# Memory attention and a gated MLP on one core: the attention transposes of pairs 1 to 3 done on VectorE from 32x32 blocks

## The chip, the cores and the metric

One NeuronCore of a Trainium2 chip. The metric is device time in microseconds (us) of one execution: TensorE (PE in the profile, with its weight loads as PEld), VectorE (DVE), ScalarE (ACT), GpSimd (POOL) and SyncE (SP, which issues the DMAs here) run side by side and wait for each other by semaphores.

## The reference, cut to what matters

```python
# q, k, v: [8, 8, 576, 64]   phi: [8, 8, 576, 32]   (batch, head, sequence, .)
a = exp(phi - max(phi, axis=2));  a = a / (sum(a, axis=2) + 1e-9)
k_m = einsum('bhsm,bhsd->bhmd', a, k)            # 32 memory slots per head
v_m = einsum('bhsm,bhsd->bhmd', a, v)
scores = q @ k_m.T / 8
attn = exp(scores - max);  attn = attn / (sum + 1e-9)        # [.., 576, 32]
x = (attn @ v_m)  as [4608, 512]                  # heads side by side
xn = x / sqrt(mean(x*x) + 1e-6) * rms_g
out = (silu(xn @ w_gate) * (xn @ w_val)) @ w_out  # 512 -> 1536 -> 512
```

## The kernel before, in words

The 8 batches are 4 pairs (`pr` 0 to 3). `x` is never formed: the weights are first multiplied by `v_m` (`vw_steps`, tile vp), and the result is multiplied by the normalised attention weights themselves (`gv_steps`, tiles pg and pv, three products of high and low halves for precision); silu and product follow, and `out_steps` multiplies by w_out into po and adds into the output tile acc. The MLP runs as 24 units of (pair, sixth of the 1536 columns), each in two slices: pair 0's first four sixths, then pairs 0 and 1 mixed, then pairs 2 and 3. These matmuls are the main stream on TensorE, from some 80 us on.

For each later pair (1 to 3) the attention has to be made ready beside that stream, in two stages:

- `attend_steps(pr, s)`, four per pair (`s`: two heads of both batches). `fetch` (L660) loads q with four DMAs, 64 partitions each, rows of 64 floats, a token on a partition. `turn` transposes 9 blocks of 128x128 on TensorE against the identity (L671, tile qtp, in runs of 4, 4 and 1), and ScalarE copies each run from PSUM to qT (L677). `score` multiplies by `k_m` (L689, tile S); max, subtraction, exponential, sum and division follow on VectorE, ScalarE and GpSimd; `put` (L730) writes the 128x576 weights to a scratch tensor in HBM with one DMA.
- `x_steps(pr)`. `fetch` (L935) loads the scratch back in three pieces of 4, 4 and 1 tiles of 64 tokens (tile ain). `turn` transposes two 128x128 blocks of each tile on TensorE (L763, tile tp, 18 per pair), `copy` brings them to the tile at, on ScalarE or VectorE by a bit list `ON_SCALAR` (L773). Then per tile `mm` (L855, xp) and `square` (L867), which reads both xp and the rows ain, give the mean of squares; `fin` makes the reciprocal root on VectorE, `spread` brings it across (L783, rp) and scales at (L791), and ScalarE and GpSimd split at into ath and atl, which `gv_steps` reads.

Pair 0 takes another way (`q_steps`, `score_steps`, L585, and L763 with the tile first) that needs no scratch. The PSUM tag "o" (two banks) holds qtp, S, tp, xp, rp and also po of the main stream. The SBUF tags qr, qT, ex of the pool `sl` have one buffer each; `x_steps` uses the same three for its pieces.

Everything is cut into some 2940 small steps (`parts`), and the list `ISSUE` at the top of the file, made by a planner, says in which order they are issued. Each engine and SP's queue work in that order, so a step's place in the list is its place in the queue of its engine; there is no other priority. SP waits at a DMA until its buffer is free, and all that is listed behind it waits with it.

Of the kernel before, what the change touches and what calls it, by code (L numbers as in the profile page):

```python
# [28 lines left out]
ON_SCALAR = (21, 28, 14, 13)  # L29

ISSUE = [
    34, 36, 27, 35, 28, 33, 10, 0, 11, 229, 12, 1, 13, 2, 14, 3, 15, 4, 30, 5, 17, 29, 16, 18, 6, 898, 7, 41,
    19, 8, 20, 31, 9, 21, 22, 42, 32, 23, 43, 905, 24, 25, 44, 48, 37, 58, 26, 45, 59, 46, 49, 230, 39, 38,
    243, 75, 899, 115, 900, 40, 76, 47, 50, 51, 240, 902, 77, 60, 903, 53, 231, 52, 61, 232, 908, 85, 242, 54,
    62, 906, 86, 55, 923, 95, 65, 63, 87, 241, 66, 64, 68, 907, 67, 96, 909, 70, 56, 127, 910, 930, 78, 88,
    901, 948, 79, 116, 97, 80, 904, 913, 89, 69, 57, 81, 98, 90, 105, 82, 118, 91, 83, 233, 71, 119, 84, 99,
    117, 234, 106, 92, 151, 100, 120, 93, 101, 235, 94, 107, 152, 139, 72, 108, 102, 924, 128, 109, 153, 110,
    129, 103, 130, 121, 73, 111, 104, 140, 131, 112, 236, 154, 925, 132, 113, 122, 155, 114, 265, 133, 123,
    156, 279, 237, 141, 134, 142, 124, 165, 143, 157, 135, 144, 933, 125, 136, 126, 74, 171, 145, 164, 244,
    163, 137, 158, 138, 166, 172, 245, 911, 146, 266, 147, 173, 159, 169, 238, 912, 246, 239, 1270, 174, 277,  # L40
    148, 247, 170, 175, 276, 1271, 149, 167, 931, 150, 278, 926, 927, 248, 1273, 176, 168, 160, 177, 928, 196,
    202, 195, 197, 249, 932, 161, 162, 198, 250, 934, 200, 252, 929, 251, 203, 1272, 267, 178, 199, 268, 253,
    201, 179, 254, 269, 184, 255, 935, 916, 270, 914, 936, 180, 185, 204, 256, 181, 188, 937, 207, 1274, 205,
    182, 949, 915, 1295, 257, 917, 183, 206, 190, 258, 918, 191, 259, 189, 192, 955, 919, 261, 271, 260, 186,
    263, 1276, 262, 264, 208, 272, 187, 193, 1279, 951, 273, 280, 950, 194, 1275, 1281, 281, 1277, 1280, 1278,
    274, 209, 920, 275, 210, 1296, 211, 216, 952, 217, 282, 1282, 212, 214, 953, 1298, 218, 223, 213, 973,
    954, 283, 215, 219, 445, 221, 1297, 224, 220, 222, 921, 225, 226, 227, 228, 956, 1286, 284, 285, 958,
    1299, 957, 286, 959, 1285, 974, 287, 960, 1290, 1287, 980, 961, 976, 1310, 1283, 975, 1289, 289, 1288,
    290, 288, 1301, 977, 1291, 978, 1312, 446, 291, 1300, 938, 979, 293, 447, 292, 1292, 448, 1302, 1304, 449,
    294, 981, 450, 1314, 464, 451, 982, 1293, 295, 984, 296, 1338, 985, 983, 939, 1284, 452, 963, 297, 1339,  # L50
    1315, 1294, 986, 1303, 453, 1306, 1305, 1340, 941, 299, 1341, 454, 987, 1307, 300, 455, 940, 1308, 1342,
    298, 1311, 942, 465, 943, 1343, 466, 1313, 998, 944, 1316, 456, 1363, 966, 1317, 457, 1345, 1309, 467,
    945, 1344, 469, 1348, 946, 483, 458, 1357, 470, 459, 1318, 1347, 999, 460, 947, 1320, 461, 468, 462, 964,
    1322, 965, 1321, 463, 1346, 967, 968, 1326, 1000, 1359, 1005, 1323, 1002, 1001, 1353, 1003, 1364, 1023,
    1004, 1324, 1349, 962, 1366, 922, 1327, 969, 1354, 471, 1319, 1365, 1350, 1367, 1355, 1325, 1356, 1006,
    472, 474, 1008, 1007, 1358, 522, 1009, 1026, 1010, 1368, 1351, 473, 1030, 1011, 1360, 1378, 1370, 475,
    1024, 476, 484, 1012, 1025, 1372, 485, 1027, 486, 1361, 1028, 488, 1406, 487, 988, 1029, 489, 502, 1330,
    1352, 477, 1328, 1331, 1362, 1031, 478, 1407, 1334, 1329, 479, 480, 1409, 481, 989, 1332, 1335, 1032, 482,
    1033, 1408, 1336, 991, 990, 1333, 992, 993, 1369, 1337, 1034, 1048, 1373, 1035, 493, 994, 1371, 1013,
    1410, 490, 1374, 301, 1375, 1383, 491, 1036, 995, 492, 1380, 1411, 1376, 494, 996, 1037, 970, 1379, 1049,  # L60
    503, 1381, 1413, 971, 1382, 1051, 495, 507, 1431, 1050, 972, 1016, 1377, 1384, 1415, 997, 1014, 1385, 508,
    1015, 504, 505, 1052, 1386, 1412, 1017, 1053, 1388, 1055, 1054, 496, 1416, 506, 1018, 1432, 1390, 1073,
    1019, 1421, 1387, 1417, 1056, 1414, 497, 1426, 1434, 1058, 498, 1389, 499, 1418, 500, 1433, 1419, 1422,
    1423, 1074, 1057, 1425, 501, 1059, 1392, 1060, 1427, 1076, 1391, 1080, 1061, 1435, 1098, 1424, 1420, 1474,
    1428, 1393, 512, 1075, 1475, 509, 513, 1077, 1446, 514, 1081, 1078, 1396, 1083, 1038, 1079, 1436, 1082,
    510, 511, 1397, 1398, 1084, 1085, 515, 1394, 1063, 1086, 1477, 516, 1062, 1399, 1437, 517, 518, 1402,
    1448, 1395, 519, 1039, 1476, 1438, 1400, 1439, 520, 1478, 1087, 1064, 1403, 1066, 1441, 1040, 1429, 1065,
    1483, 1042, 521, 1043, 1440, 1041, 1067, 1404, 1401, 1442, 1443, 523, 1068, 1102, 548, 1044, 1447, 1088,
    1479, 561, 1430, 1045, 1451, 1444, 1449, 1481, 1445, 302, 1450, 524, 1046, 1452, 1480, 1020, 525, 1489,
    1103, 1021, 1047, 1405, 528, 1482, 526, 1453, 1022, 529, 1499, 1454, 527, 1104, 1105, 1484, 1106, 1485,  # L70
    1500, 1107, 1458, 1069, 1486, 1109, 530, 1459, 1108, 1091, 1490, 1501, 1089, 1456, 1491, 1502, 1487, 1503,
    1494, 1488, 531, 1112, 1457, 532, 1090, 534, 1092, 1493, 533, 535, 1093, 549, 1495, 555, 1455, 550, 1127,
    1504, 556, 312, 1094, 1492, 553, 1496, 551, 1100, 1497, 536, 1542, 554, 537, 1110, 538, 552, 539, 1460,
    540, 541, 1543, 542, 1111, 1506, 543, 544, 1545, 545, 1508, 546, 1461, 1128, 557, 1498, 1510, 559, 1113,
    1509, 558, 1129, 562, 1114, 1505, 563, 1134, 1115, 564, 547, 560, 1116, 1544, 1462, 1507, 565, 566, 314,
    567, 578, 1511, 1463, 1514, 1512, 579, 1513, 1464, 1546, 580, 1472, 582, 581, 1137, 1130, 568, 1131, 1135,
    1465, 1516, 1473, 1468, 569, 1132, 570, 1117, 1133, 1466, 313, 1136, 571, 1469, 572, 1470, 573, 574, 575,
    1138, 1518, 1070, 1515, 1071, 1520, 1095, 1519, 576, 577, 1139, 1467, 1096, 1142, 1471, 584, 1517, 303,
    1567, 1521, 304, 1522, 585, 1524, 1568, 1152, 305, 583, 1569, 1570, 1526, 1120, 1525, 1571, 1140, 588,
    1528, 586, 1527, 589, 1141, 590, 1529, 1610, 587, 591, 306, 1530, 307, 592, 594, 593, 1118, 1557, 1143,  # L80
    1531, 1144, 1558, 595, 1523, 1547, 1534, 308, 1562, 315, 309, 1532, 1146, 1549, 1147, 1145, 1119, 1559,
    1551, 1156, 1121, 337, 1122, 1560, 1181, 1123, 1535, 1553, 1548, 1561, 1550, 1533, 1552, 1563, 1576, 1554,
    1555, 316, 1611, 1556, 1572, 1157, 1612, 1613, 1573, 310, 1574, 1614, 317, 311, 1564, 1635, 338, 1578,
    1565, 318, 1577, 1566, 319, 1582, 351, 1148, 320, 321, 1586, 348, 322, 324, 325, 323, 350, 1575, 1588,
    1579, 1587, 326, 1580, 1097, 327, 329, 1615, 328, 1584, 1581, 349, 330, 1583, 332, 331, 1072, 1585, 1619,
    333, 1589, 1636, 339, 1616, 340, 1638, 341, 1637, 334, 335, 1184, 342, 1630, 336, 343, 1617, 1159, 1540,
    1639, 1536, 1541, 344, 1618, 1158, 1538, 1160, 345, 346, 1625, 1590, 1539, 1101, 347, 1537, 1620, 1099,
    1161, 352, 373, 1678, 1627, 1621, 1163, 1182, 1622, 353, 1210, 1623, 1640, 1624, 1644, 354, 1183, 1646,
    1185, 1626, 1591, 1186, 1629, 1628, 1171, 1187, 355, 1642, 1154, 1679, 356, 357, 1654, 596, 358, 360,
    1166, 361, 359, 1641, 362, 1681, 363, 365, 1592, 364, 1680, 1682, 1606, 1643, 1593, 1631, 1632, 1598,  # L90
    1607, 1645, 1599, 1600, 1647, 1594, 1601, 1633, 366, 1634, 1595, 1650, 1596, 1652, 368, 1164, 367, 1597,
    1703, 369, 1648, 370, 371, 1604, 1649, 1165, 1651, 1605, 372, 597, 1653, 1655, 1167, 598, 1162, 599, 1683,
    600, 1168, 1602, 1656, 672, 1169, 1704, 1685, 1705, 1693, 1603, 1657, 1174, 601, 1608, 615, 602, 1706,
    1707, 1687, 1684, 1188, 1689, 1609, 1170, 1746, 1686, 1149, 1658, 1150, 603, 1172, 606, 604, 1695, 1688,
    1124, 1151, 605, 607, 1698, 1125, 608, 1690, 616, 1697, 1659, 609, 1708, 617, 610, 618, 1694, 619, 611,
# [1160 lines left out]
```

## Time and profile before

| what | value |
|---|---|
| median of 3 runs (lowest, highest) | 824.86 us (822.37, 826.59) |
| the profiled execution | 823.65 us, span of its instructions 821.9 us |
| busy share of the span | PE 96%, PEld 82%, DVE 57%, ACT 45%, POOL 29% |
| DMA packets, bytes | 98622, 119.99 MB |

The page gives busy times by engine, the chain of work that ended last (followed back from the end through what each piece waited for), groups of instructions by line, and DMA issues. The trace answers by window, by line, by tile, and in order of time. "x4" is a count; "idle" is the time an engine stood still before an instruction.

### The profile page before, as it was taken

What the parts mean: (1) busy time and instruction counts of PE and PEld (TensorE: products, weight loads), DVE (VectorE), ACT (ScalarE), POOL (GpSimd) and SP (SyncE); (2) the same over time, 40 slices, a digit from 0 to 9 for tenths busy, and PEclk for the clock granted to TensorE, in tenths of its full rate; (3) what the DMA queues carried; (4) which work ended last, traced back from release to release, by engine and by line L of the source; (5) the groups of instructions that cost most, each with busy time, mean ns of one, the idle gap of its engine ahead of it and who ended that gap; (6) DMA issues with size and microseconds to landing.
All of it is one profiled execution on the core that took longest, in us unless ns stands there. A gap on an engine that the chain in (4) does not pass through costs nothing.

```text
span 821.9 us, 19112 instructions
## 1 busy us (share of the span) xinstructions
PE 787.4 (96%) x7930; PEld 670.8 (82%) x7930; DVE 466.9 (57%) x1048; ACT 366.2 (45%) x704; POOL 238.3 (29%) x203
## 2 busy tenths in 40 slices
PE   3769999999999999999999999999999999999998
PEld 2657878887888888888888888888888888888886
DVE  5688677988763565566546353456544431443443
ACT  1657788654556654332435346532332333332221
POOL 0143545435432333222422212130422122221211
PEclk9789999999999999999999999999999999999999
DMA  9953797756383743554146461741231242131114
GB/s 323 372 179 106 186 256 234 246 189 211 124 295 73 200 143 88 152 173 137 53 136 211 141 159 44 182 141 52 78 110 57 92 155 98 45 116 52 53 28 152
DMA packets 98622, 119.99 MB, mean 146 GB/s; under 512 B 47204, under 2 KB 63976, under 8 KB 98536
## 3 DMA queue, kind: packets, MB, share of 16 engines
q1 hardware_dynamic: 98536, 118.78, 46.6%
q8 instruction: 62, 1.02, 0.5%
q14 instruction: 24, 0.20, 0.1%
HBM read 93.19 MB, written 25.56 MB: 144 GB/s over the span
## 4 chain that ended last, share of the span: by engine, by line
PE 84%; DMA 6%; ACT 3%; DVE 3%; issue 2%; SPq 1%; POOL 0%; ACTq 0%; DVEq 0%; POOLq 0%
PE po L1151 34%; PE pv L1094 17%; PE pg L1094 17%; PE vp L1059 5%; PE kvp L463 2%; PE xp L855 2%; DMA kvs<-in_k_dram 1%; PE S L689 1%; PE qtp L671 1%; PE tp L763 1%; DMA ol<-od 1%; DMA qr<-in_q_dram 1%; DMA phis<-in_phi_dram 1%; DMA raw<-in_moe_w_gate_dram 1%; DMA raw<-in_moe_w_val_dram 1%
## 5 line engine op out<-in xcount | busy, mean ns | idle before, releaser
L1125 POOL TENSOR_TENSOR hl<-hf,hh 128x512 fp32r<-128x512 f32 (+1 forms) x84 | 118.4, 1412 | 334.5 <-ACT hh L1120 329.1
L1162 DVE TENSOR_TENSOR acc<-po,acc 128x512 f32<-128x512 f32 x180 | 123.0, 687 | 114.1 <-PE po L1151 113.6
L1151 PE MATMUL po<-oh,hh 128*128 128x512 f32 x432 | 174.0, 403 | 1.6 <-DVE acc L1162 0.8
L1151 PE MATMUL po<-ol,hh 128*128 128x512 f32 x432 | 171.4, 397 | 0.2 <-DMA ol<-od 0.2
L1151 PE MATMUL po<-oh,hl 128*128 128x512 f32 x432 | 170.7, 395 | 0.0
L1110 DVE TENSOR_TENSOR hf<-pv,sg 128x256 f32<-128x256 f32 (+1 forms) x192 | 85.0, 453 | 127.8 <-PE pv L1094 89.8
L1105 ACT ACTIVATE sg<-pg 128x256 f32<-128x256 f32 (+1 forms) x192 | 77.8, 412 | 169.4 <-PE pg L1094 131.6
L1120 ACT CAST hh<-hf 128x512 fp32r<-128x512 f32 (+1 forms) x96 | 64.8, 675 | 91.5 <-DVE hf L1110 85.0
L1151 PEld LDWEIGHTS po<-oh,hh 128*128 128x128 f32 x432 | 81.3, 188 | 23.0 <-DVE acc L1162 2.5
L1151 PEld LDWEIGHTS po<-oh,hl 128*128 128x128 f32 x432 | 81.2, 188 | 19.5
L1151 PEld LDWEIGHTS po<-ol,hh 128*128 128x128 f32 x432 | 81.4, 188 | 14.3 <-DMA ol<-od 0.5
L1094 PE MATMUL pv<-ath,xh 128*128 128x256 f32 (+1 forms) x384 | 87.7, 309 | 0.5 <-DVE atl L842 0.5
L1094 PE MATMUL pg<-ath,xh 128*128 128x320 f32 (+1 forms) x384 | 86.4, 306 | 0.6 <-ACT sg L1105 0.6
L1074 DVE TENSOR_TENSOR xl<-vp,xh 128x512 fp32r<-128x512 f32 x96 | 64.9, 684 | 30.5 <-ACT xh L1076 30.0
L1094 PE MATMUL pg<-ath,xl 128*128 128x320 f32 (+1 forms) x384 | 81.4, 293 | 0.0
L1094 PE MATMUL pv<-ath,xl 128*128 128x256 f32 (+1 forms) x384 | 81.4, 293 | 0.0
L1094 PE MATMUL pv<-atl,xh 128*128 128x256 f32 (+1 forms) x384 | 81.3, 293 | 0.0
L1094 PE MATMUL pg<-atl,xh 128*128 128x320 f32 (+1 forms) x384 | 81.3, 293 | 0.0
L1076 ACT CAST xh<-vp 128x512 fp32r<-128x512 f32 x96 | 54.4, 587 | 43.5 <-PE vp L1059 18.8
L1094 PEld LDWEIGHTS pv<-ath,xh 128*128 128x128 f32 x384 | 63.1, 188 | 12.9 <-issue 4.8
L1094 PEld LDWEIGHTS pg<-ath,xh 128*128 128x128 f32 x384 | 62.9, 188 | 10.2 <-issue 3.2
L1094 PEld LDWEIGHTS pv<-atl,xh 128*128 128x128 f32 x384 | 61.4, 188 | 0.0
(126 smaller groups left out, 1086.1 us busy)
## 6 DMA issues: line engine op xcount, KB each, us to landing
wc<-wd SPq DMA_DIRECT2D x36, 512.0 KB, 5.5
oh<-od SPq DMA_DIRECT2D x36, 256.0 KB, 3.7
ol<-od SPq DMA_DIRECT2D x36, 256.0 KB, 4.3
out_dram<-acc SPq DMA_DIRECT2D x36, 256.0 KB, 2.8
qr<-in_q_dram SPq DMA_DIRECT2D x48, 144.0 KB, 4.3
raw<-in_moe_w_gate_dram SPq DMA_DIRECT2D x12, 512.0 KB, 4.8
raw<-in_moe_w_val_dram SPq DMA_DIRECT2D x12, 512.0 KB, 4.3
raw<-in_moe_w_out_dram SPq DMA_DIRECT2D x12, 512.0 KB, 4.5
```

The lines of the kernel that those rows point to most:

```text
L463: nc.tensor.matmul(st["kvp", b][cc][to, 0:128], e_of(b)[rows, hp, c, :], st["kv", b, hp][rows, :, cols], start=(c == 0), stop=(c == NT - 1),)
L855: nc.tensor.matmul(xp[64 * j:64 * j + 64, P * cc:P * cc + P], d["at"][:, t, cc, 64 * j:64 * j + 64], gb[:, j, cc], start=True, stop=True,)
L1059: nc.tensor.matmul(vp[32 * g:32 * g + 32, flip(b, cc), cc, :], vm[pr][rows, b, hp, 32 * (g % 2):32 * (g % 2) + 32], w[rows, hp, :], start= ...
L1074: V.tensor_tensor(out=xl[:, k], in0=src, in1=xh[:, k].bitcast(F32), op=ALU.subtract)
L1076: nc.scalar.copy(xs[i][0][:, k], src)
L1094: nc.tensor.matmul(pt[:, :N], l[:, flip(b, cc), cc, half * P:half * P + P], r[:, b, cc, t0:t0 + n, :].rearrange("p t x -> p (t x)"), start ...
L1105: nc.scalar.activation(sg[:, :N], acts[gi, b, 0][:, :N], AF.Silu)
L1110: V.tensor_tensor(out=acts[gi][:, :, b, :], in0=acts[gi, b, 1][:, :N].rearrange("p (t x) -> p t x", x=64), in1=acts[gi, b, 2][:, :N].rearr ...
L1120: nc.scalar.copy(hh, acts[gi].rearrange("p t b x -> p t (b x)"))
L1125: (V if gi and i < 12 else nc.gpsimd).tensor_tensor(out=hl, in0=acts[gi].rearrange("p t b x -> p t (b x)"), in1=hsplit[i, gi][0].bitcast(F ...
L1151: nc.tensor.matmul(po, l[:, tt, :], r, start=(m == 0), stop=(m == 5))
L1162: V.tensor_tensor(out=accs[key], in0=pt[0], in1=accs[key], op=ALU.add)
```

## The change

For pairs 1 to 3 no block of q and of the attention weights is transposed on TensorE any more:

- q is loaded by eight DMAs per `attend_steps`, each into 32 partitions, in runs of 32 floats, one step per group of 32 partitions (four steps). Two VectorE transposes of 128x576, which turn every 32x32 block by itself, write qT; the runs were laid so that the blocks come out where the 128x64 operand of `score` needs them. The nine TensorE transposes and three ScalarE copies are gone.
- `put` is three DMAs, one for each piece, and the scratch is three tensors for each pair.
- `x_steps` loads every piece twice: by four DMAs of 32 partitions in runs of 32 floats (`blocks`), which one VectorE transpose (128x1024, 128x1024, 128x256) turns into at, and by one DMA as rows, for `square`. Both take the same tag with its one buffer, so the rows wait until the blocks are turned. The 18 TensorE transposes and five copies are gone.
- Pair 0 is unchanged (`ON_SCALAR` is its value alone). `ISSUE` is another list throughout, of 2953 steps for 2938.

```diff
-        def fetch():
-            d["q"] = qr = sl.tile([P, NT, 2, 64], F32, tag="qr", name=f"qr{pr}_{s}")
+        def fetch(g):
+            def f():
+                if g == 0:
+                    d["q"] = sl.tile([P, 2, 2 * NT, 32], F32, tag="qr", name=f"qr{pr}_{s}")
+                h, half = divmod(g, 2)
+                for j in range(2):
+                    load(
+                        d["q"][32 * g:32 * g + 32, j],
+                        q[2 * pr + j, 2 * s + h].rearrange("(r x) d -> r x d", r=32)[:, :, 32 * half:32 * half + 32],
+                    )
+            return f
+
+        def turn():
+            d["qT"] = sl.tile([P, NT, 2, 64], F32, tag="qT", name=f"qT{pr}_{s}")
             for j in range(2):
-                for h in range(2):
-                    load(
-                        qr[64 * j:64 * j + 64, :, h, :],
-                        q[2 * pr + j, 2 * s + h].rearrange("(p c) d -> p c d", c=NT),
-                    )
...
+                V.transpose(
+                    out=d["qT"][:, :, j].rearrange("p t (r b) -> p b t r", b=2),
+                    in_=d["q"][:, j].rearrange("p (b t) c -> p b t c", b=2),
+                )
...
-        def put():
-            load(
-                a_dram[pr][:, :, 64 * s:64 * s + 64],
-                d["ex"].rearrange("p (t h) m -> p t (h m)", h=2),
-            )
+        def put(t0, n):
+            def f():
+                load(
+                    a_dram[pr, t0][:, :, 64 * s:64 * s + 64],
+                    d["ex"][:, 2 * t0:2 * t0 + 2 * n].rearrange("p (t h) m -> p t (h m)", h=2),
+                )
+            return f
...
+        def fetch(tag, t0, n):
+            x = {}
+            def blocks(g):
+                def f():
+                    if g == 0:
+                        x["b"] = sl.tile([P, 4, 2 * n, 32], F32, tag=tag, name=f"ab{pr}_{t0}")
+                    load(
+                        x["b"][32 * g:32 * g + 32].rearrange("p b c m -> p (b c) m"),
+                        a_dram[pr, t0].rearrange("(r b) t m -> r (b t m)", b=4).rearrange(
+                            "r (x m) -> r x m", m=P)[:, :, 32 * g:32 * g + 32],
+                    )
+                return f
+            def vturn():
+                V.transpose(
+                    out=d["at"][:, t0:t0 + n].rearrange("p t c (r b) -> p b (t c) r", b=4), in_=x["b"],
+                )
+            def rows():
+                a = sl.tile([P, n, 256], F32, tag=tag, name=f"ain{pr}_{t0}")
+                load(a, a_dram[pr, t0])
+                for k in range(n):
+                    srcs[t0 + k] = a[:, k]
+            return [blocks(g) for g in range(4)], vturn, rows
...
-            if fetch and t % 4 == 0:
-                steps.append(fetch(t))
-            if t % 2 == 0:
+            if pr and t % 4 == 0:
+                steps += fetch(("qr", "qT", "ex")[t // 4], *PIECES[t // 4])
+            if not pr and t % 2 == 0:
                 steps += [turn(t), copy(t)]
```

## Rows read from the trace of the kernel before

**Rows 1.** The page: busy us by engine; the chain by engine, by line.
```profile
PE 787.4 (96%) x7930; PEld 670.8 (82%) x7930; DVE 466.9 (57%) x1048; ACT 366.2 (45%) x704; POOL 238.3 (29%) x203
...
PE 84%; DMA 6%; ACT 3%; DVE 3%; issue 2%; SPq 1%; POOL 0%; ACTq 0%; DVEq 0%; POOLq 0%
PE po L1151 34%; PE pv L1094 17%; PE pg L1094 17%; PE vp L1059 5%; PE kvp L463 2%; PE xp L855 2%; DMA kvs<-in_k_dram 1%; PE S L689 1%; PE qtp L671 1%; PE tp L763 1%; DMA ol<-od 1%; DMA qr<-in_q_dram 1%; DMA phis<-in_phi_dram 1%; DMA raw<-in_moe_w_gate_dram 1%; DMA raw<-in_moe_w_val_dram 1%
```

**Rows 2.** Windows: stretch, its us, busy us of each engine, PEclk, DMA share, GB/s.
```profile
0.00:60.00 60.00, 36.42 (x865) 28.30 (x866) 41.23 (x139) 27.02 (x55) 12.12 (x22) 0.88 0.86 299
80.00:200.00 120.00, 115.51 (x1069) 98.27 (x1069) 97.89 (x224) 83.35 (x155) 55.99 (x43) 1.00 0.74 221
160.00:200.00 40.00, 39.17 (x359) 32.97 (x357) 35.66 (x91) 19.88 (x38) 18.43 (x15) 1.00 0.63 218
200.00:400.00 200.00, 199.86 (x2033) 172.04 (x2024) 120.58 (x256) 97.08 (x180) 64.62 (x55) 1.00 0.50 153
```

**Rows 3.** Groups by line and form: count, then busy us, mean ns, idle before.
```profile
L671 PE MATMUL qtp<-ident,qr 128*128 128x128 f32 x108 | 17.3, 273 | 0.4 <-DMA qr<-in_q_dram 0.4
L763 PE MATMUL tp<-ident,ain 128*128 128x128 f32 x54 | 7.8, 272 | 0.0
...
L677 ACT COPY qT<-qtp 128x512 f32<-128x512 f32 x24 | 14.1, 587 | 15.7 <-PE qtp L671 15.7
L773 ACT COPY at<-tp 128x512 f32<-128x512 f32 x10 | 5.8, 587 | 8.7 <-PE tp L763 8.5
...
L773 DVE COPY at<-tp 128x512 f32<-128x512 f32 x6 | 4.1, 689 | 0.7 <-PE tp L763 0.7
L773 DVE COPY at<-tp 128x256 f32<-128x256 f32 x2 | 0.8, 424 | 0.8 <-PE tp L763 0.8
```

**Rows 4.** Timeline of PE around three runs of transposes: start us, us, instruction, count.
```profile
94.60 0.60 PE L671 MATMUL qtp<-ident,qr 128*128 128x128 f32 x4
...
95.28 0.39 PE L1094 MATMUL pg<-atl,xh 128*128 128x256 f32 x2
95.51 0.39 PE L1094 MATMUL pg<-ath,xl 128*128 128x256 f32 x2
...
98.05 0.27 PE L671 MATMUL qtp<-ident,qr 128*128 128x128 f32 x1
...
98.40 0.40 PE L1094 MATMUL pv<-atl,xh 128*128 128x256 f32 x2
...
163.43 0.60 PE L763 MATMUL tp<-ident,ain 128*128 128x128 f32 x4
...
164.10 0.39 PE L1094 MATMUL pv<-atl,xh 128*128 128x256 f32 x2
```

**Rows 5.** Groups by line on DVE that read SBUF or long rows.
```profile
L377 DVE TENSOR_REDUCE mc<-phi 128x128 f32<-128x1152 f32 x6 | 13.4, 2240 | 0.9 <-DMA phi<-in_phi_dram 0.9
...
L988 DVE TENSOR_SCALAR wex<-wex 128x512 int32<-128x512 int32 x36 | 15.8, 442 | 0.5
...
L414 DVE TENSOR_TENSOR phi<-phi,mr 128x1152 f32<-128x1152 f32 x6 | 8.1, 1343 | 1.0 <-PE mr L405 0.9
```

**Rows 6.** A window with four q loads alone, and the page's queue line.
```profile
496.00:503.00 7.00, 7.00 (x92) 5.53 (x91) 2.14 (x5) 2.04 (x6) 2.27 (x2) 1.00 0.40 84
...
q1 hardware_dynamic: 98536, 118.78, 46.6%
```

**Rows 7.** SP's timeline: issue of four q loads, a put, a read back.
```profile
154.77 0.52 SPq L730 DMA_DIRECT2D ad<-ex  x1
158.57 0.32 SPq L935 DMA_DIRECT2D ain<-ad  x1
...
496.29 2.58 SPq L660 DMA_DIRECT2D qr<-in_q_dram  x4
```

**Rows 8.** DVE's timeline: the last scaling of pair 1's tile at.
```profile
205.49 0.41 DVE L791 TENSOR_TENSOR at<-at,rp 128x256 f32<-128x256 f32 x1
```

More of the change, by code (lines that the diff above doesn't have):

```diff
@@ L26 @@
 ]
-ON_SCALAR = (21, 28, 14, 13)
+ON_SCALAR = 21
 ISSUE = [
[159 rows of a table removed]
[160 rows of a table added]
 ]
@@ L253 @@
     gb = persist.tile([P, 2, 2, P], F32, name="gb")
-    a_dram = {i: dram.tile([P, NT, 256], F32, name=f"ad{i}") for i in range(1, NP)}
+    PIECES = ((0, 4), (4, 4), (8, 1))
+    a_dram = {(i, t0): dram.tile([P, n, 256], F32, name=f"ad{i}_{t0}") for i in range(1, NP) for t0, n in PIECES}
     w_dram = {j: dram.tile([P, HP, 2, P], F32, name=f"wd{j}") for j in range(NJ)}
@@ L654, in attend_steps @@
         d = {}
-        def fetch():
-            d["q"] = qr = sl.tile([P, NT, 2, 64], F32, tag="qr", name=f"qr{pr}_{s}")
-            for j in range(2):
-                for h in range(2):
-                    load(
-                        qr[64 * j:64 * j + 64, :, h, :],
-                        q[2 * pr + j, 2 * s + h].rearrange("(p c) d -> p c d", c=NT),
-                    )
-        def turn(t0, n):
-            def f():
-                if t0 == 0:
-                    d["qT"] = sl.tile([P, NT, P], F32, tag="qT", name=f"qT{pr}_{s}")
-                d[t0] = tp = bank("o", f"qtp{pr}_{s}_{t0}")
-                for t in range(n):
-                    nc.tensor.transpose(
-                        out=tp[:, t * P:(t + 1) * P],
-                        in_=d["q"][:, t0 + t].rearrange("p h d -> p (h d)"), identity=ident,
-                    )
-            def g():
-                nc.scalar.copy(
-                    d["qT"][:, t0:t0 + n, :].rearrange("p t x -> p (t x)"), d[t0][:, :n * P]
+        def fetch(g):
[11 more added lines that the diff above has]
+            d["qT"] = sl.tile([P, NT, 2, 64], F32, tag="qT", name=f"qT{pr}_{s}")
+            for j in range(2):
+                V.transpose(
+                    out=d["qT"][:, :, j].rearrange("p t (r b) -> p b t r", b=2),
+                    in_=d["q"][:, j].rearrange("p (b t) c -> p b t c", b=2),
                 )
-            return [f, g]
         def score(t0, n):
@@ L690, in f @@
                             sp[64 * j:64 * j + 64, 64 * t:64 * t + 64],
-                            d["qT"][:, t0 + t, 64 * j:64 * j + 64],
+                            d["qT"][:, t0 + t, j],
                             st["km", 2 * pr + j][:, s, :],
@@ L727, in norm, with x_steps @@
             )
-        def put():
-            load(
-                a_dram[pr][:, :, 64 * s:64 * s + 64],
-                d["ex"].rearrange("p (t h) m -> p t (h m)", h=2),
-            )
+        def put(t0, n):
[5 more added lines that the diff above has]
+            return f
         return (
-            [fetch] + turn(0, 4) + turn(4, 4) + turn(8, 1) + score(0, 5) + score(5, 4) + [exp, [total, guard, invert, norm], put]
+            [[fetch(g) for g in range(4)], turn] + score(0, 5) + score(5, 4) + [exp, [total, guard, invert, norm], [put(t0, n) for t0, n in PIECES]]
         )
-    def x_steps(pr, a, tag_t, tag_x, fetch=None):
+    def x_steps(pr, tag_x, a=None, tag_t=None):
         tps, xps, srcs, d = {}, {}, {}, {}
@@ L772, in f @@
             def f():
-                (nc.scalar.copy if ON_SCALAR[pr] & (1 << t0 // 2) else V.tensor_copy)(
+                (nc.scalar.copy if ON_SCALAR & (1 << t0 // 2) else V.tensor_copy)(
                     d["at"][:, t0:t0 + n].rearrange("p t c x -> p (t c x)"), tps[t0][:, :256 * n]
@@ L922, in x_steps @@
             return steps + [scaled(t0) for t0 in range(0, NT, 2)]
-        for t0, n in ((0, 4), (4, 4), (8, 1)):
+        for t0, n in PIECES:
             steps += spread(t0, n)
         return steps
-    def x2(pr):
-        got = {}
-        def fetch(t):
-            def f():
-                for tag, t0, n in (("qr", 0, 4), ("qT", 4, 4), ("ex", 8, 1)):
-                    if t0 == t:
-                        a = sl.tile([P, n, 256], F32, tag=tag, name=f"ain{pr}_{t0}")
-                        load(a, a_dram[pr][:, t0:t0 + n])
-                        for k in range(n):
-                            got[t0 + k] = a[:, k]
-            return f
-        return x_steps(pr, got.get, "o", "o", fetch)
     raw, wcols, wosplit = {}, {}, {}
@@ L1201 @@
             add(q_steps(s, t0 == 0), score_steps(s, t0, n))
-    add(x_steps(0, lambda t: st["a"][:, t], "v", "g"))
+    add(x_steps(0, "g", lambda t: st["a"][:, t], "v"))
     for b in range(2, B):
@@ L1208 @@
     for pr in range(1, NP):
-        add([attend_steps(pr, s) for s in range(HP)], x2(pr))
+        add([attend_steps(pr, s) for s in range(HP)], x_steps(pr, "o"))
     for n in range(NS):
```

319 rows, old and new, of the table ISSUE are left out of this document.

## The prediction

> **What bounds the kernel now.** I read three views, in this order. First the page's busy times and its chain [rows 1]: TensorE is busy for 96% of the span and carries 84% of the chain; the reader should see that the two lines the change deletes, qtp L671 and tp L763, stand in that chain with about 1% each (the second with pair 0's share, which stays). Then the windows [rows 2]. From 0 to 60 us TensorE works 36.4 us of 60 while loads run at 299 GB/s. From 80 to 200 us it idles 4.5 us of 120, from 200 to 400 us 0.1 us of 200, at a granted clock of 1.00, the 2.4 GHz level. So behind the start a microsecond of matmul taken off TensorE is a microsecond off the time, as long as the others keep up. The same rows show how much room they have: VectorE is busy 82% of 80 to 200 us, its fullest quarter (160 to 200 us) 89%, and only 60% from 200 to 400 us; the DMA engines 74% and 50%. Pair 1 is prepared in that tight stretch, pairs 2 and 3 in loose ones. Third the timeline of TensorE around the transposes, for what one really takes there.
>
> **What is removed on TensorE.** The group rows give 108 + 54 transposes of 273 ns [rows 3], 25 us if added up; but neighbours overlap, so I take spacings. From the start of a run of four q transposes to the second gate pair behind it is 0.68 us, where such a pair alone takes 0.23: the run costs 0.45. A single one costs 0.35 - 0.23 = 0.12, a run of four from ain 0.67 - 0.23 = 0.44 [rows 4]. Per attend step two fours and a one, twelve steps: 24 x 0.45 + 12 x 0.12 = 12.2 us. Per pair 18 from ain, as four fours and a two (half of 0.44): 3 x 1.98 = 5.9 us. Sum 18.2 us. Some runs are longer because they wait; I don't count those waits as gain.
>
> **What is removed on ScalarE and VectorE.** ScalarE loses 24 + 12 copies to qT and, without pair 0's two, eight copies of 512 columns to at: 14.1 us, about 3 for the twelve short ones, 8 x 0.587 = 4.7 [rows 3]. It is not the bound and I give it no gain. VectorE loses four copies of 689 and two of 424 ns (pair 0 keeps two long ones): 3.6 us.
>
> **What is added on VectorE.** 24 transposes of 128x576, six of 128x1024, three of 128x256. No row shows one. The nearest: a one-input operation from SBUF at 442 ns for 512 columns (0.86 ns a column), a two-input one at 1343 for 1152 (1.17), a reduction with strided reading at 2240 for 1152 (1.94) [rows 5]. By columns (13,824 + 6144 + 768 = 20,736) that is 17.9, 24.2 or 40.3 us. I take 24.2, the middle one: its length is nearest to these shapes, and the other two lie on either side of it. Net +20.6 us; a third, 6.9, falls to pair 1. There VectorE would have 97.9 + 6.9 = 104.8 us of work in a stretch that shrinks by a third of 18.2 to 114: 92%, above the 89% of its fullest quarter. At 89% it would need 117.8, which is 3.8 us more than 114. ScalarE's lighter load shortens some of the same waits, so I take 2 of these 3.8 us; the bounds are 0 (VectorE at 17.9 us, or packed tighter) and 9.5 (at 40.3: 97.9 + 12.2 = 110.1, over 0.89 = 123.7, less 114). Pairs 2 and 3 sit at 60% and cost nothing: the 7 us more each lie beside the main stream's matmuls; without that cover the whole 20.6 us would show.
>
> The Trainium skill, "Vector Engine (DVE) Microarchitecture Reference", section 3.8, says that the transpose mode sustains one element a cycle and lane; with the 0.96 GHz that "Trainium Kernel Development and Optimization", section NeuronCore Architecture, gives for VectorE that is an estimate of 1.04 ns a column, 21.6 us for all. By it the sum on VectorE would be 2.6 us lighter. No run here shows it yet.
>
> **What is added on the DMA engines.** Four q loads alone (2304 packets of 256 bytes) kept them at 0.40 for 7 us: 0.40 x 7 x 16 / 2304 = 19.4 ns a packet; the mean packet takes 0.466 x 16 x 821.9 us / 98,536 = 62 ns for 1205 bytes [rows 6]. A straight line through both gives 13.7 ns for 128 bytes; bounds 9.7 (half of 19.4) and 19.4. Per pair 9216 packets of 256 bytes go, and 18,432 for q and 9216 for the blocks come, all of 128 bytes. In pair 1's stretch: 0.74 x 120 = 88.8 us busy, minus 11.2, plus 27,648 x 13.7 ns / 16 = 23.7: 101.3 us of 114, 89%. At 19.4 ns it is 111, full. That they still fit is why I cost them at nothing; what hides them is that each load is issued well ahead of its use.
>
> The Trainium skill, "DMA: Bandwidth & Descriptors", section Specifications, wants 512 bytes or more for full rate. The trace agrees in direction: 13 bytes per ns and engine at 256 bytes, 19 for the mean packet. This rule speaks against the change; what it would do is the slower rival below.
>
> **What is added on SP's queue.** Four q loads take 2.58 us of issue [rows 7], so eight take 5.2; a put of 0.52 becomes at most 1.6; twelve block loads per pair, between 0.32 (a read back) and 0.65 each, 4 to 8 us. For pair 1: 10 + 4 + 6 = 20 us of the 120. Behind each such group stand weight loads (raw, wc, oh, ol) for the main stream; they come later by up to 5 us, and are listed further ahead than that.
>
> **What is moved, and the new waits.** Between pair 1's last put and its matmul xp stand now: block loads, the turn, and the row loads, which wait for the turn because both use one buffer; SP stands still there with whatever is listed behind. Before, the last put was issued at 154.8, the first read back at 158.6 [rows 7], and the last scaling of at came at 205.5 [rows 8]. Counting matmuls of both lists at the spacings above, 51 us of TensorE work lay between the last put and the first matmul that reads pair 1's result, and 46 lie there now. The added latency (issue about 6, turn 2.4, a second landing of some 4) fits into what was slack. Pairs 2 and 3 have their result tens of microseconds before it is read, in either list. The start is re-ordered too (q of pair 0 is loaded before phi of batch 2); no row tells which way that goes: zero, give or take 4 us.
>
> **The sum.** 823.65 (the profiled execution) - 18.2 + 2 = 807.4; it lay 1.2 us under the median of the runs, so 824.86 - 16.2 = 808.7. I say 808.5.
>
> **Rivals.**
> 1. VectorE becomes the bound of pair 1's stretch (its transposes stride at 1.94 ns): 9.5 us come back instead of 2, 816. For it: 89% is the most that a stretch of it shows. Against: it idles elsewhere mostly behind TensorE, whose matmuls come sooner now. Chance 0.14.
> 2. Pair 1's result is late: the double loading through one buffer and SP's longer queue take the 46 us and some 15 more, so that TensorE waits; the gain is nearly eaten, 824. This is also how it looks if the transposes were never what set the end. For it: SP's order is strict, and the loads behind a waiting one wait too. Against: 46 us of other work lie in between. Chance 0.09.
> 3. Slower: the DMA engines saturate between 80 and 200 us because a run of 128 bytes costs more than one of 256. The stretch is full at (114 - 77.6) / 1.728 = 21 ns a packet; the whole gain is gone at 32 and the result is slower from 34 on. At twice the q row, 38.8 ns, the engines need 77.6 + 67 = 144.6 us for 114: 31 come back, 836. Against it: the 256-byte row lies well on the line of cost by bytes, and blocks come from consecutive addresses. Chance 0.06.
> 4. Better than forecast: the waits in and around the transposes go too, and the re-ordered start idles less: 798. Chance 0.07.
>
> **How the numbers follow.** The forecast has 0.64 (its own range 802 to 814). About 0.5%, 4 us, is what a measurement here can tell from no change. Faster: 0.64 + 0.14 + 0.07 = 0.85; same: rival 2, 0.09; slower: 0.06. The range runs from 799 to 822 and takes in the first rival and half of the second.
>
> **What would show it.** Right: L671 and the tp of ain are gone with 162 matmuls, TensorE still idles under 8 us from 80 to 200 us, VectorE's transposes average near 0.7 us (576 columns), DMA packets rise by 55,000, and the DMA share of 80 to 200 us stays under 0.9. Wrong: TensorE waits for VectorE's xl, hf or acc in that stretch by more than 8 us (rival 1), the first gate matmul of pair 1 waits for ath or atl (rival 2), or weight loads land late at a DMA share near 1 (rival 3).

## The result and the profile after

| | median us (lowest, highest, runs) | profiled execution: its time, span |
|---|---|---|
| before | 824.19 (822.37, 826.59, 4) | 823.65, 821.9 |
| changed | 811.07 (808.99, 816.03, 4) | 811.83, 810.0 |

The ratio is 0.9844 (95% interval 0.9812 to 0.9877): 13 us faster. The page of the changed kernel, busy time by engine, DMA packets and the queue that SP feeds, answers to [rows 1, 6]:

```profile
PE 774.4 (96%) x7768; PEld 657.3 (81%) x7768; DVE 487.3 (60%) x1075; ACT 350.3 (43%) x659; POOL 238.6 (29%) x203
...
DMA packets 155647, 123.53 MB, mean 153 GB/s; under 512 B 104228, under 2 KB 121000, under 8 KB 155560
...
q1 hardware_dynamic: 155560, 122.32, 52.2%
```

TensorE has 162 matmuls fewer, VectorE 20.4 us more work, and 57,025 packets came on top. The queue's time grew by (0.522 x 810.0 - 0.466 x 821.9) x 16 = 637 us. With the 27,648 packets of 256 bytes that went (at 19.4 ns, [rows 6]) the 82,944 of 128 bytes cost (637 + 536) / 82,944 = 14.1 ns each, if the other packets took what they took before; 13.7 was the estimate. The windows of the changed kernel answer to [rows 2]:

```profile
60.00:80.00 20.00, 16.86 (x298) 12.60 (x299) 16.52 (x53) 12.16 (x26) 5.80 (x6) 0.74 0.51 179
80.00:200.00 120.00, 115.81 (x1143) 97.32 (x1142) 103.73 (x231) 80.67 (x148) 55.99 (x44) 0.99 0.81 209
180.00:200.00 20.00, 17.56 (x190) 13.26 (x188) 18.75 (x60) 8.32 (x15) 8.86 (x7) 1.00 0.82 274
```

From 80 to 200 us TensorE idles 4.2 us (4.5 before), and the DMA engines are at 0.81, not full. But from 180 to 200 us it idles 2.4 us and VectorE is busy for 94%. The same 20 us in the kernel before, where TensorE idles 0.8 us:

```profile
180.00:200.00 20.00, 19.18 (x149) 15.85 (x147) 17.73 (x49) 8.14 (x16) 8.65 (x7) 1.00 0.59 202
```

What TensorE waited for longest, first in the changed kernel, then before, both from 180 to 220 us (us in total, times, longest):

```profile
PE xp L882 <- DVE ssq L894: 1.3, 3, 1.0
PE rp L810 <- DVE at L818: 1.1, 1, 1.1
PE rp L810 <- DVE u L926: 1.0, 1, 1.0
PE po L1164 <- DVE at L818: 0.5, 1, 0.5
```

```profile
PE po L1151 <- DVE acc L1162: 0.8, 1, 0.8
```

The four lines of the changed kernel, 3.9 us, are waits for pair 1's squares, reciprocal roots and scalings. SP's timeline of the changed kernel shows why these come so close together [rows 7]: the last blocks and then the rows. Below it is what SP itself waited for, from 150 to 200 us.

```profile
166.92 5.44 SPq L786 DMA_DIRECT2D ab<-ad  x7
...
180.21 5.48 SPq L800 DMA_DIRECT2D ain<-ad  x2
```
```profile
SPq L971 <- DVE wex L1008: 8.6, 4, 4.1
SPq L800 <- DVE at L794: 5.3, 2, 4.6
```

VectorE's timeline: the turns, and the last scaling, which was at 205.49 us before [rows 8]. Then the first xp matmuls of pair 1, in the changed kernel and before.

```profile
173.81 2.07 DVE L794 STREAM_TRANSPOSE at<-ab 128x1024 f32<-128x1024 f32 x1
183.30 2.04 DVE L794 STREAM_TRANSPOSE at<-ab 128x1024 f32<-128x1024 f32 x1
...
207.02 0.42 DVE L818 TENSOR_TENSOR at<-at,rp 128x256 f32<-128x256 f32 x1 [0.82 <-PE rp L810]
```
```profile
189.41 1.09 PE L882 MATMUL xp<-gb,at 128*64 128x128 f32 x16
```
```profile
165.52 1.09 PE L855 MATMUL xp<-gb,at 128*64 128x128 f32 x16
```

The first row load is issued 6 us behind the start of the first turn. SP stood still for 4.1 us of that at a weight load listed ahead of it, which waited for VectorE, and then 4.6 us before the second row load, which waited for the second turn: that is the one buffer. So the first xp matmul comes 24 us later than before, and 18 us lie between it and the last scaling, where there were 40.

The new operation itself, by groups of form:

```profile
L674 DVE STREAM_TRANSPOSE qT<-qr 128x576 f32<-128x576 f32 x24 | 17.2, 755 | 0.0
...
L794 DVE STREAM_TRANSPOSE at<-ab 128x1024 f32<-128x1024 f32 x6 | 12.2, 2034 | 0.0
...
L794 DVE STREAM_TRANSPOSE at<-ab 128x256 f32<-128x256 f32 x3 | 1.9, 633 | 0.0
```

31.3 us, where 24.2 were taken. To see where the time goes, the main stream serves as a clock: each of its matmuls (vp, pg, pv, po) gets its spacing (the time from its start to the next one's) as weight, and for equal sums one reads from both traces when that much was done. The table gives that time in the kernel before and how much later (+) or sooner (-) each other kernel is there. They are single profiled executions, worked out from all rows of TensorE; the last four columns belong to experiments below (old start: the changed kernel with the start of before; old list: the order of before).

| before, us | changed | old start | old start, q not turned | old list, q on VectorE | old list, q not turned |
|---|---|---|---|---|---|
| 80.1 | +6.9 | +2.5 | +1.7 | +1.1 | +1.7 |
| 174.5 | -2.6 | -6.8 | -7.8 | +5.4 | +5.1 |
| 225.1 | +2.1 | -2.3 | -3.4 | +5.7 | +5.2 |
| 319.2 | -0.7 | -5.0 | -6.6 | +1.9 | +2.4 |
| 429.7 | -4.0 | -8.3 | -9.9 | +1.9 | +2.4 |
| 550.8 | -10.9 | -15.5 | -17.0 | +1.9 | -1.4 |
| 760.1 | -11.6 | -16.3 | -17.8 | +1.8 | -1.4 |

Changed kernel, down its column: in this execution 6.9 us are lost before the stream runs; pair 1 (80 to 225) gives 4.8, pair 2 (225 to 430) 6.1 and pair 3 (430 to 760) 7.6, together 18.5.

The rows at 174.5 and 550.8 us can't be read by themselves, because matmuls that are not of the main stream stand at other places in the two lists. At 174.5 us the kernel before had done 32 of pair 1's 72 xp matmuls (two runs of 1.09 us) and the changed one none. So of the 9.5 us that seem gained by then, and of the 4.7 that seem lost from there to 225, 2.2 are only work that was moved; some 2.5 us are lost. In the same way the row at 550.8 lies among pair 3's xp matmuls, and the end of pair 3 is read at 760.

### The profile page after: what moved, and what is told of

The parts are those of the page before. It is cut to its first block, busy times and chain, and to the rows that moved or that the text cites. A ratio compares the mean times of both kernels' runs of the same rounds, so it can differ in the third digit from the quotient of the medians.

```text
span 810.0 us, 18918 instructions
## 1 busy us (share of the span) xinstructions
PE 774.4 (96%) x7768; PEld 657.3 (81%) x7768; DVE 487.3 (60%) x1075; ACT 350.3 (43%) x659; POOL 238.6 (29%) x203
## 4 chain that ended last, share of the span: by engine, by line
PE 75%; DVE 4%; DMA 2%; ACT 2%; issue 1%; SPq 0%; POOL 0%; ACTq 0%; POOLq 0%; DVEq 0%
PE po L1164 33%; PE pv L1107 16%; PE pg L1107 16%; PE vp L1072 5%; PE xp L882 1%; PE kvp L465 1%; PE S L686 1%; DMA raw<-in_moe_w_val_dram 1%; DMA raw<-in_moe_w_out_dram 1%; DMA ab<-ad 1%; DVE acc L1175 1%; DVE at L794 1%; ACT xh L1089 0%; DVE wex L989 0%; PE rp L810 0%
## 5 line engine op out<-in xcount | busy, mean ns | idle before, releaser
L1164 PEld LDWEIGHTS po<-oh,hl 128*128 128x128 f32 x432 | 81.2, 188 | 19.5
L1164 PEld LDWEIGHTS po<-ol,hh 128*128 128x128 f32 x432 | 81.4, 188 | 13.7
L1107 PE MATMUL pv<-ath,xh 128*128 128x256 f32 (+1 forms) x384 | 85.7, 304 | 0.0
L1107 PEld LDWEIGHTS pg<-ath,xh 128*128 128x128 f32 x384 | 63.6, 189 | 13.7 <-issue 5.0
L1107 PEld LDWEIGHTS pg<-atl,xh 128*128 128x128 f32 x384 | 61.4, 188 | 0.7 <-DVE atl L869 0.7
```

The source lines that it names most:

```text
L1107: nc.tensor.matmul(pt[:, :N], l[:, flip(b, cc), cc, half * P:half * P + P], r[:, b, cc, t0:t0 + n, :].rearrange("p t x -> p (t x)"), start ...
L1164: nc.tensor.matmul(po, l[:, tt, :], r, start=(m == 0), stop=(m == 5))
```

## The experiments

Theory A: the 18.2 us of TensorE are had behind the start, and what is missing is lost in the re-ordered start. Theory B: it is lost to VectorE's slow turns and the small packets between 80 and 200 us. "Old" is the order of the kernel before, "new" that of the changed one. `ISSUE` is a list of some 2950 numbers, so edits of it are given in words.

**The changed kernel again**, without an edit, as the standard for the others.

> The changed kernel as it is, beside the same runs of the kernel before. Both theories: about 811 us, ratio 0.984. Theory A (18 us are saved behind the start, some 7 us are lost in the re-ordered start, before the main stream runs) adds: the main stream's first matmuls come 7 to 10 us later than before, and the spread from run to run comes with the clock of the first 90 us. Theory B (the start's loss is made up by itself, and what is missing to 18 us went to VectorE's slow block transposes and to the small packets between 80 and 200 us) expects no such tie.

810.66 us (806.25 to 813.05), ratio 0.983 (0.9804 to 0.9855). The granted clock of the whole run is 0.993 and 0.991 in the two runs near 806 us and 0.985 to 0.987 in the four at 810 to 813. Single runs of one kernel lie up to 8 us apart, so smaller differences between single runs mean little.

The profiled execution of this repeat took 806.25 us, 5.6 less than the 811.83 of the table, and by the same reading of the main stream it is 1.2 us late at 80.1 us (6.9 in the table) and 17.1 us early at 760.1 (11.6). So both gain the same behind the start, 18.3 and 18.5 us, and what sets them apart is lost before the main stream runs. The stretch from 20 to 35 us, changed and changed again (the third number from the end is the granted clock):

```profile
20.00:35.00 15.00, 9.96 (x226) 8.84 (x224) 5.32 (x17) 4.99 (x12) 1.22 (x2) 0.51 1.06 379
```
```profile
20.00:35.00 15.00, 9.95 (x235) 8.74 (x235) 6.88 (x22) 6.27 (x14) 1.23 (x2) 0.77 1.07 379
```

The kernel before has 0.66 there. From 60 to 80 us the granted clock is 0.74 in the changed kernel, 0.94 in its repeat and 0.95 before.

**The start alone, in either kernel.** First the changed kernel with the old start, then the old kernel with the new start, then the changed kernel with only its first 24 loads in old order.

```diff
-ISSUE = [new: start] + [new: rest]
+ISSUE = [old: all up to the first q load of pair 1] + [new: rest]
```

> The changed kernel, but the steps up to the first q load of pair 1 are issued in the order of the kernel before; the rest keeps the changed kernel's order. Theory A: 824.2 - 18.5 = 805 to 806 us, 5 to 7 faster than the changed kernel. Theory B: 811, within 1 us of the changed kernel, since pair 1's stretch is as full as before.

```diff
-ISSUE = [old: start] + [old: rest]
+ISSUE = [new: start] + [old: rest]
```

> The kernel before (TensorE transposes and all), with its steps up to the first q load of pair 1 issued in the changed kernel's order (without its early loads of a later weight column and of phi of batch 4). Theory A: 824.2 + 6 = 830 us (828 to 832). Theory B: 824 to 825, no change.

```diff
-ISSUE = [new: 24 loads first in the list, among other steps]
+ISSUE = [the same places, filled with the same 24 loads in old order]
```

> The changed kernel with only the first 24 load steps after the fixed ones in the order of the kernel before (phi of batch 2 and the gate and value weights among the q loads, not behind all eight); all other steps keep the changed order. If the lost microseconds of the start come from late loads (theory A, first form): 805 to 807 us. If they come from the order of the compute steps (theory A, second form): 811 or more. Theory B: 811.

Measured: 812.34 us, ratio 0.9841 (0.9816 to 0.9865), no gain; 828.69 us, ratio 1.0051 (1.003 to 1.0071), so 4.2 us lost; 810.1 us, ratio 0.9827 (0.9805 to 0.9849), no change. The second says that the new start costs 4 us, the first does not. At its seam two loads of the new order came to lie right ahead of pair 1's q loads, and TensorE was busy for only 16.76 of the 20 us from 80 on, with 2.3 lost in one wait (for ScalarE's gram). That the seam hid a gain is a guess at this point. So it was run again with the two put further back:

```diff
-ISSUE = [old start] + [a weight's read-back, phi of batch 4, q loads of pair 1, ...]
+ISSUE = [old start] + [q loads of pair 1, ...], the two loads 360 and 110 steps later
```

> As the run with the old start, but the two early loads (a weight column that is read 130 us later, and phi of batch 4) are issued later, so that pair 1's first q loads don't queue behind them. If the old start is worth its 4.4 us to the changed kernel too and only that seam hid it: 824.3 - 18 = 806 to 807 us. If the order of the start is worth nothing here: 810 to 812.

806.45 us (804.18 to 810.33), ratio 0.9778 (0.975 to 0.9806): the fastest kernel of this study that leaves nothing out, and 4.2 us under the changed one, though the two intervals just touch. So both kernels lose about 4 us to the new start; in the old kernel that is clear of the noise, in the changed one it is at its edge, and the two loads were moved with it. TensorE's wait for VectorE's maximum over phi goes with it; the rows are from the kernel before, the changed one, the changed one again, old with new start, new with old loads, and new with old start:

```profile
PE mt L384 <- DVE mc L377: 4.9, 3, 3.0
```
```profile
PE mt L386 <- DVE mc L379: 9.1, 3, 5.5
```
```profile
PE mt L386 <- DVE mc L379: 8.5, 3, 5.0
```
```profile
PE mt L380 <- DVE mc L373: 8.6, 3, 5.0
```
```profile
PE mt L382 <- DVE mc L375: 8.5, 3, 5.0
```
```profile
PE mt L382 <- DVE mc L375: 4.9, 3, 3.0
```

The wait follows the start's order of steps, 3.6 to 4.2 us longer with the new one, and the order of the first 24 loads alone does not take it away. That is the size of the loss. But the repeat of the changed kernel has the same wait and was only 1.2 us late at 80.1 us, at a higher granted clock than the execution that was 6.9 late. In one execution the wait and the clock stand together; the runs don't separate them.

**VectorE's turns made shorter.** They write runs of 32 floats instead of every second (q) or fourth float (attention weights). What is left out is the order of the tokens, so the result is not the reference's.

```diff
-out=d["at"][:, t0:t0 + n].rearrange("p t c (r b) -> p b (t c) r", b=4)
+out=d["at"][:, t0:t0 + n].rearrange("p t c (b r) -> p b (t c) r", b=4)
-out=d["qT"][:, :, j].rearrange("p t (r b) -> p b t r", b=2)
+out=d["qT"][:, :, j].rearrange("p t (b r) -> p b t r", b=2)
```

> The changed kernel, but VectorE's transposes write their blocks as runs of 32 floats and not with a step of two or four floats; the loads are unchanged, so tokens come out permuted within a batch. Theory V (the step of the written floats sets the 2.03 us of a block turn, and VectorE's work near pair 1's input is what TensorE waits for): the 1024-column turn falls to about 1.2 us, the 576-column one to about 0.7, TensorE's waits from 180 to 220 us fall from 4 to 2 us, time 808. Rival (a turn takes its time by columns, or TensorE waits for the late row loads): rows unchanged, or rows shorter and the same 810 to 811.

```profile
L670 DVE STREAM_TRANSPOSE qT<-qr 128x576 f32<-128x576 f32 x24 | 17.1, 752 | 0.0
L790 DVE STREAM_TRANSPOSE at<-ab 128x1024 f32<-128x1024 f32 x6 | 7.4, 1233 | 0.0
L790 DVE STREAM_TRANSPOSE at<-ab 128x256 f32<-128x256 f32 x3 | 1.3, 420 | 0.0
```
```profile
PE xp L878 <- DVE ssq L890: 1.3, 3, 1.0
PE rp L806 <- DVE at L814: 1.0, 1, 1.0
PE rp L806 <- DVE u L922: 1.0, 1, 1.0
PE po L1160 <- DVE at L814: 0.5, 1, 0.5
```

810.32 us, ratio 0.9822 (0.9794 to 0.9849). The long turns fell from 2034 to 1233 ns and the time did not move, nor did the four waits at 180 to 220 us (second fence). Pair 1's share of what was saved is only 1.8 us, less than the time alone can tell; the waits are what speaks. The turns of q, which did not get shorter here, follow below.

**Half of the change, in the new list.** First q on VectorE and the attention weights back on TensorE, then the reverse; the transposes and copies stand where the turn stood.

```diff
-... "x1.turn (VectorE)" ...
+... "x1.T0", "x1.copy0", "x1.T2", "x1.copy2" ...
```

> The changed kernel with the attention weights again read back once as rows and transposed on TensorE (54 transposes, copies on ScalarE and VectorE); q stays on VectorE. Theory V: TensorE gets 5.9 us more work, but the 4 us of waits from 180 to 220 us go with the block turns and the double loading: 811 to 813. Rival (the waits have another cause): 816 to 817.

```diff
-... "at1.0.turn (VectorE)" ...
+... "at1.0.T0", "at1.0.copy0", "at1.0.T4", "at1.0.copy4", "at1.0.T8", "at1.0.copy8" ...
```

> The changed kernel with q again loaded in four DMAs a step and transposed on TensorE (108 transposes, ScalarE's copies); the attention weights stay on VectorE. By the spacings 12.2 us come back on TensorE: 823. If VectorE's q turns or q's small packets cost something, less comes back: 819 to 822.

826.66 us (ratio 1.0027, 1.001 to 1.0044) and 852.89 us (1.0338, 1.0306 to 1.037): 16 and 42 us more than the changed kernel, where the transposes' spacings are 5.9 and 12.2. Both expectations missed. From 80 to 600 us TensorE waits 6.4 us for the copies to at (L767) in the first. Its longest waits in the second:

```profile
PE qtp L670 <- ACT qT L676: 10.4, 15, 1.8
PE po L1166 <- ACT qT L676: 3.3, 8, 0.6
PE qtp L670 <- DVE acc L1177: 2.7, 5, 0.9
```

Placed back to back, runs of transposes wait for the copies of those ahead of them, in the two PSUM banks that they share with po. These waits and the transposes' spacings make 12 of the 16 us and 29 of the 42; the rest is not accounted for. The two runs tell what a place in the list is worth, not what a half of the change is worth.

**Half of the change, in the old list.** q on VectorE at the old places, the attention weights on TensorE as before.

```diff
-"at1.0.fetch", ..., "at1.0.T0", "at1.0.copy0", ..., "at1.0.T8", "at1.0.copy8"
+"at1.0.fetch0", "at1.0.fetch1", "at1.0.fetch2", "at1.0.fetch3", ..., "at1.0.turn (VectorE)"
```

> One part alone, with nothing planned anew: the order of the kernel before, in which only q goes to VectorE (four block loads at the place of the one load, the turn at the place of the first transpose); the attention weights stay on TensorE. If the prediction's step holds that a spaced run of transposes costs TensorE its own columns and their gaps and nothing else, this part is worth 12 x (eight transposes and the wide one, taken at their spacing) = 12.2 us: 824.5 - 12.2 = 812.3 us, at or beside the changed kernel, although half of the change is left out and because no start is re-ordered. Theory B (small packets and VectorE's turns give time back) says 816 or more, since all the turns of q are there. Under 809 us would say that the transposes held more than their spacing.

825.98 us (823.7 to 827.21), ratio 1.0011 (0.9993 to 1.0029): nothing of the 12.2 us is there, and 812.3 was expected. So the turning was taken out of this kernel, and of the fastest one. What is left out is the arrangement of q's numbers, so the result is not the reference's. The blocks of q also take turns in two buffers here, that of qT being free:

```diff
-d["q"] = sl.tile(..., tag="qr", ...)
+d["q"] = sl.tile(..., tag=("qr", "qT")[s % 2], ...)
...
 def turn():
-    d["qT"] = sl.tile(...)
-    V.transpose(out=..., in_=...)
+    pass
...
-d["qT"][:, t0 + t, j],
+d["q"][:, j, 2 * (t0 + t):2 * (t0 + t) + 2].rearrange("p x c -> p (x c)"),
```

> The kernel of the last run but one (order of before, q in 32x32 blocks, 825.98 us) with the turning of q left out altogether: the scores are taken straight from the blocks as loaded (in two buffers that take turns), so TensorE has no transposes of q, VectorE no turns, ScalarE and VectorE no copies of q; the attention weights stay on TensorE. What is left out is the arrangement of q's numbers. Theory A2 (the transposes of before stood where TensorE would otherwise wait for the steps between its matmuls, so in the order of before their 12.2 us can't be had): 820 to 826 us, with TensorE's waits on sg, hf and acc as in the run with turns. Theory B2 (it was VectorE's 24 turns, 18.4 us in its list, that ate the 12 us): near 812 us and those waits gone.

> The fastest kernel so far (changed kernel with the old start, 806.45 us) with the turning of q left out in the same way: scores straight from the blocks. What is left out is the arrangement of q's numbers; the turns of the attention weights stay. It bounds what VectorE's 24 turns of q cost in the order planned anew. The prediction's step (hidden behind TensorE's matmuls): 805 to 807 us. If the turns cost the time of a VectorE that is waited for: up to 18 us less, under 802 us.

In the old list 822.79 us, ratio 0.9977 (0.9961 to 0.9993); in the new one 805.57 us, ratio 0.9768 (0.9742 to 0.9794). Without VectorE's 24 turns of q the time is 3.2 us less in the old list (2.8 by the ratios, whose intervals touch) and 0.9 us less in the new one (inside the intervals). So Theory B's VectorE part falls: with short block turns or without turns of q the new list has the same time within the noise. Nor is there anything left for the small packets, which no run took out alone: read like the table, one execution of each of the seven kernels with the new list (the changed one twice, three with another start or load order, and the two with other turns) gives 16.2 to 19.5 us from 80.1 to 760.1 us, 18.5 in the middle, where 18.2 were priced. That is Theory A.

What does cost in the old list is seen from 80 to 200 us, with TensorE's window and longest waits of the kernel that doesn't turn q:

```profile
80.00:200.00 120.00, 109.02 (x1028) 91.03 (x1027) 95.58 (x217) 78.08 (x142) 53.56 (x41) 1.00 0.76 216
```
```profile
PE pv L1097 <- DVE hf L1113: 3.8, 3, 1.7
PE po L1154 <- ACT acc L1163: 2.0, 1, 2.0
PE pg L1097 <- ACT sg L1108: 1.6, 2, 1.4
```

TensorE idles 11.0 us there, 6.5 more than before. ScalarE waits for raw weights, 80 to 160 us, the longest line of the kernel before and then of this one:

```profile
ACT wex L972 <- DMA raw<-in_moe_w_out_dram: 3.0, 2, 2.3
```
```profile
ACT mi L987 <- DMA raw<-in_moe_w_out_dram: 7.1, 2, 3.7
```

All such lines together are 8.9 us before and 13.5 here. SP's timeline shows two of those loads late, first before, then here:

```profile
99.62 1.31 SPq L660 DMA_DIRECT2D qr<-in_q_dram  x2
...
103.33 0.59 SPq L730 DMA_DIRECT2D ad<-ex  x1
105.04 0.38 SPq L958 DMA_DIRECT2D raw<-in_moe_w_val_dram  x1
...
111.90 0.38 SPq L958 DMA_DIRECT2D raw<-in_moe_w_val_dram  x1
```
```profile
99.69 5.82 SPq L660 DMA_DIRECT2D qr<-in_q_dram  x5
...
106.74 2.02 SPq L718 DMA_DIRECT2D ad<-ex  x3
108.87 0.39 SPq L961 DMA_DIRECT2D raw<-in_moe_w_val_dram  x1
...
115.74 0.38 SPq L961 DMA_DIRECT2D raw<-in_moe_w_val_dram  x1
```

The more numerous q loads and puts, in one clump, push the weight loads behind them back by 3.8 us. That the clump is the cause of TensorE's idle time is argued from these rows and not shown. Against it: the kernel that turns q on VectorE has the same loads as late and loses as much by 174.5 us (table), but its ScalarE waits for raw weights only 10.6 us there, 1.7 more than before. And the new list has clumps too, six q loads in a row for each of the first two steps, here the second:

```profile
99.49 6.01 SPq L665 DMA_DIRECT2D qr<-in_q_dram  x6
```

The other reading is that the transposes filled places where TensorE would have waited anyway. It can't be all: then the stretch would be as long as before, and it became 3.4 us longer in this execution (from +1.7 to +5.1 in the table). How the rest is shared was not separated. Pairs 2 and 3 of the kernel without turns fit the clump: from 200 to 400 us the DMA share is 0.53, and q gives 2.8 us in pair 2 and 3.8 in pair 3, near the 4.1 that four steps have by spacing (table, last column). With VectorE's turns it is 3.8 and 0; pair 3 then shows waits of 1.5 us for hf and 0.8 for acc, and a granted clock of 0.84 from 520 to 530 us.

**Pair 1's chain spread out**, to win the 4 us of waits at 180 to 220 us, on top of the old start.

```diff
-..., xp, square, xp, square, ... (nine pairs close together), fin, fin, ...
+..., xp, xp, other matmuls, square, square, xp, ... the first ones earlier; fin steps between other VectorE steps
```

> The kernel with the old start (806.5 us measured) with one stretch changed: the matmuls of pair 1's attention weights, their squares and the steps behind them stand earlier and further apart in the order, between matmuls of the other work, with the same loads and turns. If the 4 us of TensorE waits at 176 to 224 us come from the squeezed chain behind the late rows, they go: 802 to 804 us. If they come from VectorE being too busy there (0.94 of 180 to 200), it stays at 806 to 807 us, with the waits on VectorE somewhere else in the stretch.

813.7 us, ratio 0.9864 (0.9828 to 0.99): 7 us worse than without. The waits, 150 to 240 us:

```profile
PE vp L1068 <- DVE xl L1083: 3.0, 1, 3.0
PE rp L806 <- DVE rinv L928: 3.0, 1, 3.0
```

Three of the four waits are gone (the 0.5 us of po stays) and two longer ones stand in their place, behind VectorE steps that were put elsewhere. Both expectations of this run missed: what the squeezed chain costs stays open. A second buffer, which would let rows and blocks come at once, was not tried.

## Why the prediction was right, and where not

**TensorE's 18.2 us, by spacing.** Right, in the changed kernel: 18.5 us were had behind the start (16.2 to 19.5 with the other kernels of the new list), pair by pair 4.8, 6.1 and 7.6 where 6.1 each were priced (a third of 18.2). Why pair 3 gave 1.5 us more is not shown. The argument behind it was too wide. "Behind the start a microsecond of matmul taken off TensorE is a microsecond off the time, as long as the others keep up": in the old list the others did not keep up in pair 1's stretch, and a kernel with 12.2 us fewer transposes stood at 825.98. The new order was priced only where it could hurt; it is part of what makes the saving.

**2 us given back in pair 1's stretch.** Near in size for that stretch (4.8 us gained, 6.1 - 2 = 4.1 forecast), wrong in kind, and over all three pairs nothing is given back (18.5 for 18.2). VectorE's turns were to crowd the stretch: they took 31.3 us, the upper middle of the bounds, and it made no difference that can be told from the noise, as the shorter turns and the missing turns of q show. What pair 1 is short of lies by the rows in the chain behind the late row loads (3.9 us of waits, and some 2.5 us lost from 174 to 225), the place that the second rival named, at a small part of its price; the run that spread this chain did not win it back.

**SP's queue, hidden.** "They come later by up to 5 us, and are listed further ahead than that" holds for the new list alone. In the old one two of them were 3.8 us late, and ScalarE waited for raw weights 4.6 us more than before, where no turn of q was left.

**The DMA engines, nothing.** Right: 0.81 of 80 to 200 us, 14.1 ns a packet. The third rival is out. The argument against it was empty, though: that the 256-byte row lies on the line of cost by bytes is so for any line drawn through it.

**The start, zero give or take 4 us.** The mis-sized term: it costs 4.2 us in either kernel by the medians, just past the end of its bounds. With it the sum would have been 812.7; the 811.07 measured lie 1.6 under that, about the 2 us that were not given back. So that the forecast of 808.5 lies within 3 us of the result is in part luck: two errors had opposite signs.

**VectorE's turn, near 0.7 us at 576 columns.** 755 ns, 1.31 ns a column. With runs of 32 floats 256, 576 and 1024 columns took 420, 752 and 1233 ns: each further column 1.04 to 1.07 ns, and some 150 ns for each instruction besides (an estimate from these three). With every fourth float 256 and 1024 columns took 633 and 2034 ns, 1.82 ns a further column. The Trainium skill, "Vector Engine (DVE) Microarchitecture Reference", section 3.8, speaks of one element a cycle and lane, 1.04 ns a column by the estimate ahead. The traces agree for each further column written in runs of 32; a whole turn takes more, and one with every fourth float nearly twice as much a column. The measurement decides.

**Slips in the working.** 160 to 200 us is a third of the stretch, not a quarter, and the upper bound of VectorE's cost comes out as 123.7 - 114 = 9.7, not 9.5. Neither changes the forecast.

## What to carry to other kernels

In a kernel whose order is one list for all queues, price a removed instruction by its spacing, where in the new list that held within 2 us, for each pair as for all three, and ask what the list puts in its place: removing q's transposes was worth nothing in the old list, and putting transposes back to back into the new one cost 16 and 42 us for 5.9 and 12.2. Look at the loads that a change's DMA issues push back in their queue. Test a re-ordered start by itself, in both kernels, before blaming the new operations. And where one stream of matmuls is used as a clock, cut it only where the other matmuls of both lists are equally far.

## What was not expected of the hardware

A VectorE transpose of 32x32 blocks depends on the step it writes with: 128x1024 took 2034 ns with every fourth float and 1233 ns with runs of 32, while 128x576 took 755 ns with every second float and 752 with runs of 32. And one kernel's runs spread over 6.8 us (806.25 to 813.05): of the 5.6 us between its two profiled executions all were lost before the main stream, where from 20 to 35 us the granted clock was 0.51 in the one and 0.77 in the other. The clock of the whole run is a rougher sign: the six runs of the changed kernel with the old start all have 0.985 and spread over 6.0 us.
